# KV times wo in 64x64 tiles for two head groups at once, and modulation rows put beside den

## The chip, the cores and the metric

The kernel runs on one core of one Trainium2 chip. The metric is device time in microseconds (us) of one execution; lower is better. Engines are named as in the profile: PE is the matrix engine, PEld its weight loads, DVE the vector engine, ACT the scalar engine, POOL the GpSimd engine, SP the engine whose queue issues nearly all DMA transfers.

## What is computed

One transformer block on 2048 tokens of width 1024: linear attention with 32 heads of 32, and a gated feed-forward layer of width 3584, each behind a layernorm that six modulation rows (shift, scale and gate for each half) scale and shift. The reference, cut to what matters:

```
mod = silu(c) @ w_mod                      # six rows of 1024: sa ca ga sb cb gb
h = layernorm(x) * (1 + ca) + sa
q, k, v = h @ wqkv                         # 32 heads of 32
phi = lambda t: where(t > 0, t + 1, exp(t)) + 1e-6
kv  = einsum('bhsd,bhse->bhde', phi(k), v) # one 32x32 block for each head
z   = einsum('bhsd->bhd', phi(k))
num = einsum('bhqd,bhde->bhqe', phi(q), kv)
den = einsum('bhqd,bhd->bhq', phi(q), z) + 1e-6
x = x + ga * ((num / den) @ wo)
h = layernorm(x) * (1 + cb) + sb
x = x + gb * ((gelu(h @ w_gate) * (h @ w_up)) @ w_down)
```

## The kernel before

The 2048 tokens are 16 chunks of 128, in four groups of 512. The program is recorded as a list of operations for each engine. PE's and SP's lists keep the order in which the code records them; the lists of DVE, ACT and POOL are put in a new order over the first third of the kernel by `reorder`, a list planner that works with a table of costs (`COST`) by name and starts first what is due first. Operations on one engine run in their list's order, and an operation waits on semaphores for what it depends on. SP has eight lanes: a transfer waits for the transfer eight places before it.

The steps around the change:

- K and Q are computed and put through phi. V is never formed: with M = phi(K)^T h (tiles `m_tile`, L895, 8 head groups of 128 columns, three column parts each), the product KV of a head group g is M times the V weights.
- M is copied to bf16 by ACT (L900), transposed by a DMA into `mtb` (`m_t`, L703; two buffers, so the transpose of group g waits for the KV product of g-2), and multiplied with the V weights by `kv_prod` (L913, 8 matmuls of 128 columns). The result, one 128x128 matrix of which only the four 32x32 blocks on the diagonal belong to heads, is multiplied by a block mask on DVE into `KVT` (L917).
- KV times wo, `w2_pair` (L1196): for each head group, `KVT` of the group (128x128, block diagonal) is the stationary operand and 128 rows of wo the moving one, two matmuls of 512 columns into two PSUM banks. ACT copies the result to bf16, `W2` (L1198). wo itself is loaded by two transfers (`wo_load`) and multiplied beforehand by the gate row ga on DVE (`wofold`, L1202).
- The modulation rows of a later step are summed by `mod_rows` (L840): a matrix of ones as stationary operand, 32 columns wide, four row parts beside each other in the four column quarters of the array (this is what "column-tiled" means below). ACT copies the rows out and SP stores them to DRAM (`mod_store`, L849). sb and cb are read back from there with one value to a partition, `sbT` and `cbT` (L1213), 1024 values of 4 bytes each; `cb1` on DVE (L1749) adds one.
- `den` (L1223) makes the denominators of half of the tokens: 32 matmuls of 32 stationary columns, again four beside each other. DVE adds 1e-6 and takes the reciprocal, SP stores it (L1231), and `rb_load` (L1243) reads it back, spread over the 32 partitions of each head: 256 KB for each of four transfers to a half group. `pq_scale` on DVE (L1256, `pqs`) multiplies phi(Q) with it.
- `wo_mm` (L1266): phi(Q) times `W2`, 16 matmuls for a chunk; DVE adds the result to x (L1274, `x1`).
- The second layernorm's rows are transposed by DMA (L703 into `h2a` and `h2b`), modulated (L724 on DVE, L753 on ACT), and go into the feed-forward layer, which works with sums and differences of blocks (seven products in place of eight): `s_sum` (L1395, `ss`) of the activations, `t_sum` (L1415, `tp`) of the weights `wt`, products L1440.

The table `HOOK` says behind which M tile (0 to 23, `tiles`) each of these steps is recorded. After the tiles a fixed sequence mixes the first chunks of `wo_mm` with the last KV products and the last groups of `w2_pair`; SP's transfers `rb_load(1)` and `rb_load(2, (1,))` are recorded there too. `gb_rows` makes the gate row of the second half, whose stored value is read back much later.

Of the kernel before, what the change touches and what calls it, by code (L numbers as in the profile page):

```python
# [7 lines left out]
ACTF = mybir.ActivationFunctionType  # L8
ALU = mybir.AluOpType

P = 128
# [7 lines left out]
NG = 8  # L19
# [151 lines left out]
class Sched:  # L171
# [41 lines left out]
    def dma(self, stream, fn, rd=(), wr=(), deps=(), note="", overwrite_ok=False):  # L213
# [6 lines left out]
        if prev is not None:  # L220
# [4 lines left out]

    COST = {
        PE_: {"T": (0.056, 0.15), "k": (0.216, 0.15), "q": (0.216, 0.15), "v": (0.216, 0.15), "m": (0.145, 0.15), "kv": (0.056, 0.15), "den": (0.027, 0.15),
              "modr": (0.04, 0.15), "mod": (0.028, 0.15), "w": (0.216, 0.15), "wo": (0.216, 0.15), "ffn": (0.216, 0.15)},
        ACT_: {"exp": (0.5, 0.1), "sum": (1.19, 0.1), "sq": (1.28, 0.1), "xhata": (1.14, 0.1), "hmoda": (0.49, 0.1), "mcp": (0.38, 0.1), "zc": (0.13, 0.1),
               "mhi": (0.52, 0.1), "mrow": (0.4, 0.1), "wcp": (0.92, 0.1), "hraw": (0.92, 0.1), "hmodb": (0.75, 0.1), "arcp": (0.98, 0.1),  # L230
               "brcp": (0.98, 0.1), "pcp": (0.55, 0.1), "escp": (0.55, 0.1), "gelu": (0.55, 0.1)},
        DVE_: {"min": (0.34, 0.085), "add": (0.607, 0.085), "bn": (0.603, 0.085), "aggr": (0.124, 0.085), "ve": (0.07, 0.085), "xhat": (0.46, 0.085),
               "nm": (0.074, 0.085), "hmod": (0.25, 0.085), "macc": (0.66, 0.085), "mlo": (0.6, 0.085), "kvt": (0.21, 0.085), "z": (0.34, 0.085),
               "dene": (0.335, 0.085), "rden": (1.67, 0.085), "pqs": (0.6, 0.085), "wofold": (1.13, 0.085), "x": (1.14, 0.085), "ssum": (1.15, 0.085), "tsum": (1.15, 0.085), "padd": (0.62, 0.085), "yT": (0.62, 0.085)},
        POOL_: {"nmean": (0.22, 0.05), "ve": (0.22, 0.05), "rstd": (0.55, 0.05), "nm": (0.55, 0.05), "ones": (0.12, 0.05), "ssum": (2.3, 0.05), "tsum": (2.3, 0.05)},
        SP_: {"T": (1.25, 1.25), "Tb": (1.25, 1.25), "mT": (1.25, 1.25), "wm": (0.45, 2.9), "wo": (0.45, 2.7), "wv": (0.45, 1.45), "x": (0.45, 2.7), "gab": (0.45, 1.3),
              "sbT": (0.45, 1.3), "cbT": (0.45, 1.3), "rb": (0.45, 1.2), "wt": (0.45, 2.9), "wd": (0.45, 5.8), "wmg": (0.45, 2.9), "gbb": (0.45, 1.3), "rdenst": (0.45, 0.3), "mrowst": (0.45, 0.05)},
# [93 lines left out]
def bass_adaLN_cond__linear_attn_block__geglu_ffn__prompt_kernel(  # L331
# [18 lines left out]
    with ExitStack() as es:  # L350
# [195 lines left out]
        def PS(b, c0=0, c1=512):  # L546
            return ps_all[:, b * 512 + c0: b * 512 + c1]
# [241 lines left out]
        def r_hlg(j, h):  # L789
            return [(OFF_TMP + (2 * j + h) * 1024, OFF_TMP + (2 * j + h + 1) * 1024, "hlg")]  # L790
# [41 lines left out]
        def mod_rows(parts):  # L832
            for k0, n, bank, src in parts:
                o = None
                w = n * P
                for h in range(2):
                    for j in range(4):
                        ap, rng = src(k0 + j * n // 4, h)
                        ap = ap[:, j * w % 512:j * w % 512 + w]
                        o = sch.op(T, lambda e, h=h, j=j, ap=ap, bank=bank, w=w: e.matmul(  # L840
                            ps_all[32 * j:32 * (j + 1), bank * 512:bank * 512 + w], ONES[:, :], ap, start=(h == 0), stop=(h == 1)),
                            rd=rng + r_sm("ones"), pwr=(pr(bank) if h == j == 0 else ()), note=f"modr{k0}.{h}.{j}")
# [66 lines left out]
        def kv_prod(g, bank):  # L909
            i = g % 2  # L910
            o = None
            for dc in range(NDC):
                o = sch.op(T, lambda e, dc=dc: e.matmul(PS(bank, 0, P), WV[:, g, dc, :], MTB[i][:, dc, :],  # L913
                                                        start=(dc == 0), stop=(dc == NDC - 1)),
                           rd=r_wv(g) + r_mtb(i), pwr=(pr(bank) if dc == 0 else ()), note=f"kv g{g} dc{dc}")
# [274 lines left out]
            sch.op(V, lambda e: e.tensor_tensor(Z32[:], BM32[:], ZCOLS[:, :].unsqueeze(2).to_broadcast([P, NG, NH]), ALU.mult),  # L1190
                   rd=r_sm("bm32") + r_sm("zcols"), wr=r_sm("z32"), note="z32")

        def w2_pair(g, b0=6):
            for half in range(2):
                b = b0 + half
                sch.op(T, lambda e, b=b, half=half: e.matmul(PS(b), KVT[:, g, :], WO[:, g, half * 512:(half + 1) * 512], start=True, stop=True),  # L1196
                       rd=r_kvt(g, g + 1) + r_wo(g, half * 512, (half + 1) * 512), pwr=pr(b), note=f"w2 {g}.{half}")
            sch.op(A, lambda e: e.activation(W2[:, g, :], ps_all[:, b0 * 512:(b0 + 2) * 512], ACTF.Copy),  # L1198
                   prd=pr(b0) + pr(b0 + 1), wr=r_w(OFF_WK, "w2", g), note=f"w2cp{g}")

        def wofold(kc):
            sch.op(V, lambda e: e.tensor_tensor(WO[:, kc, :], WO[:, kc, :], GAB[:, :], ALU.mult), rd=r_wo(kc) + R_GAB, wr=r_wo(kc), note=f"wofold {kc}")  # L1202

        def wo_load(j):
            sch.dma(Q, lambda e: e.dma_start(WO[:, 4 * j:4 * j + 4, :], wo_v[:, 4 * j:4 * j + 4, :]),
                    wr=[t_ for g in range(4 * j, 4 * j + 4) for t_ in r_wo(g)], note=f"wo{j}")

        def mod_pass():
            assert mdone[0] >= 48 and not late
            mod_rows(((2, 4, 5, hl_src),))  # L1210
            o_r = mod_store(4, 5, MROW[1], r_2k(OFF_ROW + 2048, "mrow1"), 1)
            for dst, nt, a0 in ((SBT, "sbT", 0), (CBT, "cbT", 2)):
                sch.dma(Q, lambda e, dst=dst, a0=a0: e.dma_start(dst[:, :], scr_row[1, a0:a0 + 2, :].rearrange("a (b p) -> p (a b)", p=P)),  # L1213
                        wr=r_sm(nt), deps=[o_r], note=nt)

        HW = SGW // 2

# [43 lines left out]
        def wo_mm(c_, b0, gs):  # L1261
# [9 lines left out]
            if gs[-1] == NG - 1:  # L1271
# [38 lines left out]
        for n, (g, k) in enumerate(tiles):  # L1310
# [656 lines left out]
```

## Time and profile before

| | |
|---|---|
| median of 3 runs | 783.46 us (783.44 to 783.54) |
| the profiled execution | 783.52 us, of which the span in the trace is 781.7 |
| granted clock of PE | 1.00 |
| PE busy | 774.5 us (99%) |
| DVE, ACT, POOL busy | 641.9, 376.3, 47.0 us |
| M tiles and what is between them | 127.5 to 191.8 us of the span |
| first chunks of `wo_mm` with the last KV products | 191.8 to 200.9 us |
| the remaining chunks to 13 | 200.9 to 242.3 us |
| the feed-forward layer's first unit, with chunks 14 and 15 | 242.3 to 262.0 us |
| end of all PE work | 777.4 us |

How to read the views that are shown: the chain of waits is followed back from the last instruction, at each step to what released it, and printed in order of time; pieces stand end to end. In a timeline each row is a run of like instructions with its start, the time from its first start to its last end, engine, line, operation, tiles written and read, shapes and count, and in brackets the idle time of the engine just before it with what ended it. A matmul's own duration contains its way through the array, so the time that it costs in a row of matmuls is seen from start to start. The table by stretch gives busy time of each engine in a window, then granted clock, DMA share and GB/s. "To landing" is the time from a transfer's issue to the moment when its semaphore is complete. All times are from the start of the span.

### The profile page before, as it was taken

The numbers are of one execution on the slowest core, as the hardware profiler recorded it, in microseconds if no ns is written. First come the engines' busy times: TensorE is split into PE (matmuls) and PEld (weight loads), VectorE is DVE, ScalarE is ACT, GpSimd is POOL, SyncE is SP. The second block draws the span as 40 slices with busy tenths as digits, with TensorE's granted clock in tenths as the row PEclk, the third lists the DMA queues.
The fourth block names the chain that finished last, engine by engine and source line by source line (L and its number), as shares of the span: only waits on it lengthen the run. The fifth ranks groups of instructions, "written<-read, shape, count | busy, mean of one in ns | idle before, by whom it ended". The sixth has DMA issues, their size and how long they took to land.

```text
span 781.7 us, 10762 instructions
## 1 busy us (share of the span) xinstructions
PE 774.5 (99%) x3867; PEld 497.4 (64%) x3867; DVE 641.9 (82%) x954; ACT 376.3 (48%) x631; POOL 47.0 (6%) x126
## 2 busy tenths in 40 slices
PE   8999999999999999999999999999999999999998
PEld 4444445666445667677676767677676576677766
DVE  6699988896689877787989888888989888676767
ACT  2497743243566487778655565555555211111111
POOL 2031300000331012100000000000000000000000
DMA  9879749939999247867353866435356334444331
GB/s 289 250 166 252 156 84 260 229 70 182 216 270 248 82 128 215 226 184 214 93 152 107 246 207 180 141 102 160 94 150 218 112 115 152 145 141 123 113 128 60
DMA packets 196844, 130.22 MB, mean 167 GB/s; under 512 B 69420, under 2 KB 182324, under 8 KB 195768
## 3 DMA queue, kind: packets, MB, share of 16 engines
q1 hardware_dynamic: 196776, 129.55, 61.0%
q8 instruction: 30, 0.49, 0.3%
q14 instruction: 22, 0.18, 0.1%
q10 hardware_dynamic: 16, 0.00, 0.0%
HBM read 92.55 MB, written 23.35 MB: 148 GB/s over the span
## 4 chain that ended last, share of the span: by engine, by line
PE 97%; SPq 1%; DMA 1%; DVE 0%; issue 0%; DVEq 0%
PE ps_all L1440 45%; PE ps_all L1654 21%; PE ps_all L895 7%; PE ps_all L1266 7%; PE ps_all L931 7%; PE ps_all L880 6%; PE ps_all L1575 1%; DMA wmq<-in_w_mod_dram 1%; SPq L598 1%; SPq L603 1%; PE ps_all L913 0%; PE ps_all L1196 0%; SPq L592 0%; PE ps_all L1223 0%; PE ps_all L766 0%; PE ps_all L840 0%
## 5 line engine op out<-in xcount | busy, mean ns | idle before, releaser
L1440 PE MATMUL ps_all<-ss,tp 128*128 128x512 f32 x896 | 214.3, 396 | 0.0
L1440 PEld LDWEIGHTS ps_all<-ss,tp 128*128 128x128 f32 x896 | 168.3, 188 | 37.7 <-DVE ss L1395 0.3
L1654 PE MATMUL ps_all<-dt,sb 128*128 128x512 f32 x424 | 102.5, 398 | 0.0
L1440 PE MATMUL ps_all<-h2a,wt 128*128 128x512 bf16 x448 | 101.6, 380 | 0.0
L1463 ACT ACTIVATE ge<-ps_all 128x512 f32<-128x512 f32 x112 | 64.1, 597 | 73.8 <-DVE ps_all L1451 62.0
L1654 PEld LDWEIGHTS ps_all<-dt,sb 128*128 128x128 f32 x424 | 79.6, 188 | 18.4 <-DVE sb L1630 0.3
L1458 DVE TENSOR_TENSOR ps_all<-ps_all,es 128x512 f32<-128x512 f32 x54 | 37.5, 699 | 49.7 <-ACT es L1448 49.3
L1470 DVE TENSOR_TENSOR ys<-ge,ps_all 128x512 bf16<-128x512 f32 x112 | 74.4, 684 | 3.4 <-PE ps_all L1654 0.5
L1440 PEld LDWEIGHTS ps_all<-h2a,wt 128*128 128x128 bf16 x448 | 37.9, 97 | 57.2 <-ACT ps_all L1445 16.9
L1415 DVE TENSOR_TENSOR tp<-wt 128x1024 fp32r<-128x1024 bf16 x56 | 68.1, 1216 | 2.1 <-DMA wt<-in_B_w_up_dram 2.1
L1415 DVE TENSOR_TENSOR tp<-wt,tp 128x1024 fp32r<-128x1024 bf16 x56 | 68.2, 1219 | 0.0
L880 PE MATMUL ps_all<-wk,h1T 128*128 128x512 bf16 x248 | 56.7, 379 | 0.3 <-DVE h1T L724 0.2
L931 PE MATMUL ps_all<-h1T,wq 128*128 128x512 bf16 x256 | 56.7, 379 | 0.0
L1266 PE MATMUL ps_all<-w,pq 128*128 128x512 bf16 x256 | 56.3, 379 | 0.0
L1440 PE MATMUL ps_all<-ar,tp 128*128 128x512 f32 x224 | 55.5, 390 | 0.0
L869 ACT ACTIVATE eb<-ps_all 128x512 f32<-128x512 f32 x64 | 36.3, 593 | 37.7 <-PE ps_all L880 15.3
L1654 PE MATMUL ps_all<-wd,ya 128*128 128x512 bf16 x212 | 48.5, 380 | 0.0
L1440 PEld LDWEIGHTS ps_all<-ar,tp 128*128 128x128 f32 x224 | 42.1, 188 | 8.8
L1445 ACT ACTIVATE ps_all<-ps_all 128x512 f32<-128x512 f32 x56 | 32.6, 582 | 27.1 <-PE ps_all L1440 27.1
L931 PEld LDWEIGHTS ps_all<-h1T,wq 128*128 128x128 bf16 x256 | 24.9, 98 | 30.0
L1266 PEld LDWEIGHTS ps_all<-w,pq 128*128 128x128 bf16 x256 | 24.7, 98 | 29.9 <-ACT w L1198 0.3
L1625 ACT ACTIVATE sb<-ya 128x896 fp32r<-128x896 bf16 (+1 forms) x16 | 14.5, 913 | 58.8 <-PE ps_all L1654 58.8
(140 smaller groups left out, 977.5 us busy)
## 6 DMA issues: line engine op xcount, KB each, us to landing
wt<-in_B_w_gate_dram SPq DMA_DIRECT2D x28, 512.0 KB, 4.1
wt<-in_B_w_up_dram SPq DMA_DIRECT2D x28, 512.0 KB, 5.3
scr_y<-ys SPq DMA_DIRECT2D x28, 512.0 KB, 3.2
ya<-scr_y SPq DMA_DIRECT2D x14, 896.0 KB, 5.9
rb<-scr_rd SPq DMA_DIRECT2D x32, 256.0 KB, 6.9
wd<-in_B_w_down_dram SPq DMA_DIRECT2D x7, 1024.0 KB, 7.9
wmst<-in_w_mod_dram SPq DMA_DIRECT2D x6, 1024.0 KB, 5.7
wmq<-in_w_mod_dram SPq DMA_DIRECT2D x8, 512.0 KB, 6.8
```

The source lines that it names most:

```text
L869: sch.op(A, lambda e: e.activation(EB[i][:, :], PS(bank), ACTF.Exp), prd=pr(bank), wr=rng, note=f"{note}.exp")
L880: o = sch.op(T, lambda e, dc=dc: e.matmul(PS(bank), H1[sg][:, ci, dc, :], W_[:, dc, jg * 512:(jg + 1) * 512], start=(dc == 0), stop=(dc == ...
L895: o = sch.op(T, lambda e, c_=c_: e.matmul(PS(bank, 0, n), PK[c_][:, g * P:(g + 1) * P], xrow(c_, o_, o_ + n), start=(c_ == 0), stop=(c_ == ...
L931: o = sch.op(T, lambda e, dc=dc: e.matmul(PS(b), WQ[:, dc, qc * P:(qc + 1) * P], H1[sg][:, :, dc, :], start=(dc == 0), stop=(dc == NDC - 1 ...
L1266: last[half] = sch.op(T, lambda e, g=g, half=half: e.matmul(PS(b0 + half), PQ[sg][:, g, ci * P:(ci + 1) * P], W2[:, g, half * 512:(half + ...
L1415: sch.op(V, lambda e: e.tensor_tensor(TP[k][:], in0, in1 if k in (0, 2) else in1[:], ALU.subtract), rd=r0 + r1, wr=r_tp(k), deps=[x1_ops[7 ...
L1440: o = sch.op(T, lambda e, l_=l_, r_=r_, dc=dc: e.matmul(PS(b), l_, r_, start=fresh and dc == 0, stop=dc == ND2 - 1, skip_group_check=True) ...
L1445: sch.op(A, lambda e: e.activation(PS(BB + t), PS(BA + t), ACTF.Copy), prd=pr(BA + t), pwr=pr(BB + t), note="pcp")
L1458: sch.op(V, lambda e: e.tensor_tensor(PS(BC + t), PS(BC + t), ES[t][:, :], ALU.add), prd=pr(BC + t), rd=r_2k(OFF_ES[t], f"es{t}"), pwr=pr( ...
L1463: sch.op(A, lambda e: e.activation(GE[i][:, :], PS(b), ACTF.Gelu_apprx_tanh), prd=pr(b), wr=r_2k(OFF_GE[i], f"ge{i}"), note="gelu")
L1470: sch.op(V, lambda e: e.tensor_tensor(YS[s_][:, 2 * h:2 * h + 2, t, :], q(GE[i][:, :]), q(PS(b + 1)), ALU.mult), rd=r_2k(OFF_GE[i], f"ge{i ...
L1654: o = sch.op(T, lambda e, l_=l_, r_=r_, j=j, dst=dst: e.matmul(dst, l_[:, 0, :], r_, start=(k in (1, 5) or own is not None) and j == js[0] ...
```

## The change

Of a 128x128 `KVT` only the two 64x64 blocks on the diagonal can be other than zero. The changed kernel keeps only these. `kv_prod` masks each of the two blocks by itself on DVE and puts it into `KVT` so that the partitions 0 to 63 hold the blocks of an even group and 64 to 127 those of the odd group beside it. wo is loaded by four transfers of 64 partitions each, so that its rows lie in the same way. `w2_pair(i)` then makes two head groups at once: 8 matmuls of 64x64 tiles with 512 columns each; the two row halves of the array belong to the two groups and write to different banks, the two column halves to the two blocks of a group. It uses four banks (4 to 7) in place of two. Of the last two pairs, DVE makes the second copy to `W2` in place of ACT.

The four pairs stand behind tile 11, behind tile 17, and twice in the sequence after the tiles. The modulation rows of sb and cb (`modp`) stand directly before den0 behind tile 16, where before they stood behind tile 14; the rows of gb (`gbr`) stand directly behind den1 after tile 20, where before they stood behind tile 21, and use bank 7. The reads of `sbT` and `cbT` (`mod_in`) are recorded after `rb_load(1)` and `rb_load(2, (1,))`, where before they followed the store. The planner's cost table has new values for three names.

```diff
-              "modr": (0.04, 0.15), "mod": (0.028, 0.15), "w": (0.216, 0.15), "wo": (0.216, 0.15), "ffn": (0.216, 0.15)},
+              "modr": (0.04, 0.15), "mod": (0.028, 0.15), "w": (0.07, 0.3), "wo": (0.216, 0.15), "ffn": (0.216, 0.15)},
...
-               (DVE) "kvt": (0.21, 0.085)
+               (DVE) "kvt": (0.15, 0.085), "wcp": (1.05, 0.085)
...
         def gb_rows():
-            mod_rows(((0, 2, 5, lambda j, h: (HLG[:, j, h, :], r_hlg(j, h))),))
-            o_gb[0] = mod_store(2, 5, MRG, [(OFF_TMP + 4096, OFF_TMP + 5120, "mrg")], 2)
+            mod_rows(((0, 2, 7, lambda j, h: (HLG[:, j, h, :], r_hlg(j, h))),))
+            o_gb[0] = mod_store(2, 7, MRG, [(OFF_TMP + 4096, OFF_TMP + 5120, "mrg")], 2)
...
             pset_writer(bank, o)
-            sch.op(V, lambda e: e.tensor_tensor(KVT[:, g, :], PS(bank, 0, P), BMASK[:, :], ALU.mult), prd=pr(bank), rd=r_sm("bmask"),
-                   wr=r_kvt(g, g + 1), note=f"kvt{g}")
+            z = 64 * (g % 2)
+            for h in range(2):
+                a, gz = 64 * h, g // 2 * 2 + h
+                sch.op(V, lambda e, a=a, gz=gz: e.tensor_tensor(KVT[z:z + 64, gz, 0:64], ps_all[a:a + 64, bank * 512 + a:bank * 512 + a + 64], BMASK[a:a + 64, a:a + 64], ALU.mult),
+                       prd=pr(bank), rd=r_sm("bmask"), wr=r_kvt(gz, gz + 1), note=f"kvt{g}", overwrite_ok=True)
...
-        def w2_pair(g, b0=6):
-            for half in range(2):
-                b = b0 + half
-                sch.op(T, lambda e, b=b, half=half: e.matmul(PS(b), KVT[:, g, :], WO[:, g, half * 512:(half + 1) * 512], start=True, stop=True),
-                       rd=r_kvt(g, g + 1) + r_wo(g, half * 512, (half + 1) * 512), pwr=pr(b), note=f"w2 {g}.{half}")
-            sch.op(A, lambda e: e.activation(W2[:, g, :], ps_all[:, b0 * 512:(b0 + 2) * 512], ACTF.Copy),
-                   prd=pr(b0) + pr(b0 + 1), wr=r_w(OFF_WK, "w2", g), note=f"w2cp{g}")
+        def w2_pair(i, b0=4):
+            for hf in range(2):
+                for r in range(2):
+                    for h in range(2):
+                        b, g = b0 + 2 * r + hf, 2 * i + h
+                        sch.op(T, lambda e, b=b, g=g, h=h, r=r, hf=hf: e.matmul(ps_all[64 * h:64 * h + 64, b * 512:(b + 1) * 512], KVT[64 * r:64 * r + 64, g, 0:64],
+                               WO[64 * r:64 * r + 64, g, hf * 512:(hf + 1) * 512], start=True, stop=True),
+                               rd=r_kvt(g, g + 1) + r_wo(g, hf * 512, (hf + 1) * 512), pwr=pr(b), note=f"w2 {i}.{hf}", overwrite_ok=True)
+            for r in range(2):
+                b, g = b0 + 2 * r, 2 * i + r
+                w_, p_ = W2[:, g, :], ps_all[:, b * 512:(b + 2) * 512]
+                eng = V if i > 1 and r else A
+                sch.op(eng, lambda e, w_=w_, p_=p_, eng=eng: e.activation(w_, p_, ACTF.Copy) if eng == A else e.tensor_copy(w_, p_),
+                       prd=pr(b) + pr(b + 1), wr=r_w(OFF_WK, "w2", g), note=f"w2cp{g}")
...
         def wo_load(j):
-            sch.dma(Q, lambda e: e.dma_start(WO[:, 4 * j:4 * j + 4, :], wo_v[:, 4 * j:4 * j + 4, :]),
-                    wr=[t_ for g in range(4 * j, 4 * j + 4) for t_ in r_wo(g)], note=f"wo{j}")
+            for r in range(2):
+                wo_ops.append(sch.dma(Q, lambda e, r=r: e.dma_start(WO4[64 * r:64 * r + 64, :, j, :], wo_rows[r, :, :, j, :]),
+                                      wr=() if r else [t_ for g in range(j, NG, 2) for t_ in r_wo(g)], deps=wo_ops[-1].deps if r else (), note="woe"))
...
         def mod_pass():
-            mod_rows(((2, 4, 5, hl_src),))
-            o_r = mod_store(4, 5, MROW[1], r_2k(OFF_ROW + 2048, "mrow1"), 1)
+            mod_rows(((2, 4, 6, hl_src),))
+            o_sb[0] = mod_store(4, 6, MROW[1], r_2k(OFF_ROW + 2048, "mrow1"), 1)
+
+        def mod_in():
             for dst, nt, a0 in ((SBT, "sbT", 0), (CBT, "cbT", 2)):
                 sch.dma(Q, lambda e, dst=dst, a0=a0: e.dma_start(dst[:, :], scr_row[1, a0:a0 + 2, :].rearrange("a (b p) -> p (a b)", p=P)),
-                        wr=r_sm(nt), deps=[o_r], note=nt)
+                        wr=r_sm(nt), deps=[o_sb[0]], note=nt)
...
-        HOOK = {0: "ga", 6: "kv0", 8: "w0", 9: "kv1", 11: "w1", 12: "kv2", 14: "w2 modp", 15: "kv3 z32", 16: "den0", 17: "w3 rb0.0 rb0.1", 18: "",
-                19: "kv4", 20: "w4 den1 ps0.0", 21: "gbr", 22: "ps0.1", 23: "rb2.0"}
+        HOOK = {0: "ga", 6: "kv0", 9: "kv1", 11: "w0", 12: "kv2", 15: "kv3 z32", 16: "modp den0", 17: "w1 rb0.0 rb0.1", 18: "",
+                19: "kv4", 20: "den1 gbr ps0.0", 22: "ps0.1", 23: "rb2.0"}
...
-        E6 = list(range(6))
-        wo_mm(0, 0, E6[:5])
-        w2_pair(5)
+        wo_mm(0, 0, [0, 1, 2, 3])
+        w2_pair(2)
+        wo_mm(1, 2, [0, 1, 2])
         kv_prod(6, 4)
-        wo_mm(1, 2, E6[:5])
         kv_prod(7, 5)
-        w2_pair(6)
-        wo_mm(0, 0, E6[5:])
-        wo_mm(1, 2, E6[5:])
+        wo_mm(0, 0, [4, 5])
         rb_load(1)
         rb_load(2, (1,))
-        wo_mm(2, 4, E6[:4])
-        w2_pair(7)
-        wo_mm(2, 4, E6[4:])
+        mod_in()
+        w2_pair(3)
+        wo_mm(1, 2, [3, 4, 5])
+        wo_mm(2, 4, list(range(6)))
         for c_ in range(3):
             wo_mm(c_, 2 * c_, [6, 7])
```

More of the change, by code (lines that the diff above doesn't have):

```diff
@@ L232 @@
         DVE_: {"min": (0.34, 0.085), "add": (0.607, 0.085), "bn": (0.603, 0.085), "aggr": (0.124, 0.085), "ve": (0.07, 0.085), "xhat": (0.46, 0.085),
-               "nm": (0.074, 0.085), "hmod": (0.25, 0.085), "macc": (0.66, 0.085), "mlo": (0.6, 0.085), "kvt": (0.21, 0.085), "z": (0.34, 0.085),
-               "dene": (0.335, 0.085), "rden": (1.67, 0.085), "pqs": (0.6, 0.085), "wofold": (1.13, 0.085), "x": (1.14, 0.085), "ssum": (1.15, 0.085), "tsum": (1.15, 0.085), "padd": (0.62, 0.085), "yT": (0.62, 0.085)},
+               "nm": (0.074, 0.085), "hmod": (0.25, 0.085), "macc": (0.66, 0.085), "mlo": (0.6, 0.085), "kvt": (0.15, 0.085), "z": (0.34, 0.085),
+               "dene": (0.335, 0.085), "wcp": (1.05, 0.085), "rden": (1.67, 0.085), "pqs": (0.6, 0.085), "wofold": (1.13, 0.085), "x": (1.14, 0.085), "ssum": (1.15, 0.085), "tsum": (1.15, 0.085), "padd": (0.62, 0.085), "yT": (0.62, 0.085)},
         POOL_: {"nmean": (0.22, 0.05), "ve": (0.22, 0.05), "rstd": (0.55, 0.05), "nm": (0.55, 0.05), "ones": (0.12, 0.05), "ssum": (2.3, 0.05), "tsum": (2.3, 0.05)},
@@ L1201, in wofold @@
         def wofold(kc):
-            sch.op(V, lambda e: e.tensor_tensor(WO[:, kc, :], WO[:, kc, :], GAB[:, :], ALU.mult), rd=r_wo(kc) + R_GAB, wr=r_wo(kc), note=f"wofold {kc}")
+            sch.op(V, lambda e: e.tensor_tensor(WO[:, kc, :], WO[:, kc, :], GAB[:, :], ALU.mult), rd=r_wo(kc) + R_GAB, wr=r_wo(kc), deps=wo_ops[2 * (kc % 2) + 1:2 * (kc % 2) + 2], note=f"wofold {kc}")
+        wo_ops = []
+        WO4 = WO[:].rearrange("p (i h) d -> p i h d", h=2)
+        wo_rows = A_wo.rearrange("(i r h p) d -> r p i h d", r=2, h=2, p=64)
@@ L1208, in mod_pass @@
         def mod_pass():
             assert mdone[0] >= 48 and not late
-            mod_rows(((2, 4, 5, hl_src),))
-            o_r = mod_store(4, 5, MROW[1], r_2k(OFF_ROW + 2048, "mrow1"), 1)
+            mod_rows(((2, 4, 6, hl_src),))
+            o_sb[0] = mod_store(4, 6, MROW[1], r_2k(OFF_ROW + 2048, "mrow1"), 1)
+        o_sb = [None]
+        def mod_in():
             for dst, nt, a0 in ((SBT, "sbT", 0), (CBT, "cbT", 2)):
                 sch.dma(Q, lambda e, dst=dst, a0=a0: e.dma_start(dst[:, :], scr_row[1, a0:a0 + 2, :].rearrange("a (b p) -> p (a b)", p=P)),
-                        wr=r_sm(nt), deps=[o_r], note=nt)
+                        wr=r_sm(nt), deps=[o_sb[0]], note=nt)
```

## The prediction

> **What bounds the kernel now.** I read four views: busy times, then the chain that ended last, then the SP queue and the DMA share, then DVE's and PE's order of time where PE meets DVE.
>
> ```profile
> PE 774.5 (99%) x3867; PEld 497.4 (64%) x3867; DVE 641.9 (82%) x954; ACT 376.3 (48%) x631; POOL 47.0 (6%) x126
> ```
>
> PE is busy 99%. From the chain of waits, in order of time (start, us, what), around the edited instructions:
>
> ```profile
> 165.16 0.43 PE ps_all L1196 x2
> 165.59 0.55 PE ps_all L840 x8
> 166.14 2.43 PE ps_all L895 x16
> 168.56 0.45 PE ps_all L913 x8
> 169.01 2.32 PE ps_all L895 x16
> 171.33 0.99 PE ps_all L1223 x32
> 172.32 2.43 PE ps_all L895 x16
> ```
>
> These stand end to end, so a PE microsecond saved here is one gained here. One head group's KV times wo (L1196) costs 0.43. The column-tiled stretches cost more than their stream: the modulation rows (L840, 8 matmuls of 512 columns, four side by side, so two rounds) take 0.55 where two full-width matmuls of 512 take 0.43, and the 16 matmuls behind take 2.43, not 2.32. So a stretch costs 0.23 beyond its stream, and den (L1223) shows about the same.
>
> Whether the gain reaches the end is decided later. The SP queue's timeline:
>
> ```profile
> 173.70 0.37 SPq L1213 DMA_DIRECT2D sbT<-scr_row  x1
> 174.12 0.58 SPq L1213 DMA_DIRECT2D cbT<-scr_row  x1
> ...
> 192.09 1.25 SPq L703 DMA_TRANSPOSE mtb<-mb  x1
> 193.45 12.44 SPq L1243 DMA_DIRECT2D rb<-scr_rd  x16
> 210.76 1.24 SPq L703 DMA_TRANSPOSE h2a<-xl  x1
> ```
>
> The two small loads have an idle queue at 174; at 193 sixteen loads of 256 KB begin, and transposes and weights follow. Table by stretch (the last three columns are the granted clock, DMA share and GB/s):
>
> ```profile
> 195.00:205.00 10.00, 10.00 (x54) 4.67 (x52) 4.64 (x8) 3.14 (x4) 0.22 (x1) 1.00 1.02 230
> 205.00:214.00 9.00, 9.00 (x43) 4.09 (x42) 9.00 (x16) 6.46 (x11) 5.90 (x12) 1.00 1.01 214
> ```
>
> The DMA engines are full in both. Then DVE:
>
> ```profile
> 214.04 0.16 DVE L1749 TENSOR_SCALAR cb1T<-cbT 128x8 f32<-128x8 f32 x1
> 214.92 1.22 DVE L1274 SCALAR_TENSOR_TENSOR xall<-ps_all,xall 128x1024 bf16<-128x1024 f32 x1 [0.72 <-PE ps_all L1266]
> ...
> 225.33 1.22 DVE L1415 TENSOR_TENSOR tp<-wt 128x1024 fp32r<-128x1024 bf16 x1 [2.11 <-DMA wt<-in_B_w_up_dram]
> ...
> 251.65 1.21 DVE L1395 TENSOR_TENSOR ss<-h2a,h2b 128x1024 fp32r<-128x1024 bf16 x1
> ```
>
> and PE:
>
> ```profile
> 249.48 3.63 PE L1266 MATMUL ps_all<-w,pq 128*128 128x512 bf16 x16
> 252.92 2.12 PE L1440 MATMUL ps_all<-ss,tp 128*128 128x512 f32 x8
> ```
>
> DVE waits 2.11 for a weight transfer, then runs almost without a pause from 225.33 to 252.86, where it ends the ss that PE takes at 252.92. No room is left: what feeds DVE at 225 to 231 by DMA sets PE at 253. The first ss,tp products begin at 245.61; the second eight (245.61 + 8 x 0.225 = 247.4) need the ss ending at 246.99, a room of 0.4.
>
> **The change, part by part.** The sum is made against the profiled execution: 783.52 us, of which the span is 781.7 and 1.8 lie around it; the median of the runs is 783.46, 0.06 less.
>
> KV times wo. Removed: 8 pairs x 0.43 = 3.44. Added: 4 stretches of 8 matmuls of 64 x 64. If four run at once (two row halves into different PSUM banks, two column halves), that is two rounds of 512, as L840: 0.43 of stream + 0.23 = 0.66, times 4 = 2.64. No row has tiles of 64 rows. Bounds: 0.66 (all four at once), 1.09 (column halves only, four rounds), 1.94 (one after the other). I take 0.66, since L840 is the nearest row: four tiles, 512 columns. The larger ends are a rival below.
>
> Joint stretches. Modulation rows directly before den0, and den1 directly before the other rows, are one column mode each: 2 x 0.23 = 0.46 saved. PE's sum: -3.44 + 2.64 - 0.46 = **-1.26**. By the last KV product of the tile loop (191.4 before) the same 1.3 is already won: five pairs gone (-2.15), two stretches added (+1.32), -0.46.
>
> On loading weights, the row first: in L1223's stretch 32 loads of 128x32 go beside 32 matmuls in 0.99, and eight rounds of 256 columns are 0.85 of that, so the second load of a tile isn't in the open. The Trainium skill (TensorE: Matmul & The Clock Gate, "The mechanism") says that a weight load overlaps running matmuls only when its row group differs; den's tiles all share theirs, so the trace disagrees. By that rule the second round of each new stretch would pay a load of 0.1 in the open, PE's sum would be about -0.9, and the rival in which all is kept would end at 782.6.
>
> DVE, ACT. Each bmask product becomes two of 64x64 (nearest row 0.28 for 128x128, 8 more: between 0 and 2.2 in all), and two of the eight W2 copies move from ACT (1.02 each) to DVE (nearest row 1.22). Cover: from 192.4 to 200.9 DVE does 0.6 of work in 8.5. Behind the copies in DVE's queue stand the KVT products of groups 6 and 7: copy 193.0 to 194.2, group 7's second product ends near 195.8, the last w2 stretch wants it at 196.1. ACT's copies free the banks: kv6 wants bank 4 at 194.2, the copy ends near 194.0; chunk 2 wants it at 198.0, the copy ends near 197.8. Rooms of 0.2 to 0.3, taken as nothing; without them 0.1 to 0.5 is lost.
>
> DVE's planned order also changes: mlo7 lies between kv4's products and den1's sum. Adding the rows from dene0 on, it ends near 182.0 and PE wants it at 182.9.
>
> Queues. wo comes in four loads of 64 partitions instead of two. SP's two issues took 3.0; gab behind them is issued at 136.9. If 64 partitions load at the rate of the rb loads (1.2 per 256 KB of 32 partitions), 2 MB take 9.4 instead of about 6, gab comes 4 later, and DVE, first needing it at 140.9, has idle rows of 1.57, 1.29 and 0.98 to catch up, while the first w2 moves from 149.3 to 156.7. I take 0; the other end is 0.5.
>
> mrow1's store, rden0's store and mT4 move up with PE; the rb loads then begin near 176.5, not 177.56, so the transpose mT5 (landed 9.1 after 181.43, at 190.5) lands near 189.4, and kv5 wants it at 190.1. mT7 can go only after kv5: it lands 3.1 after its issue, near 193.9, wanted at 194.7. mrow2's store now stands before mT6, which has over 2 of room. POOL's order is unchanged.
>
> The loads sbT and cbT move behind rden0's store, mT4, the first eight rb loads, mT5, rden1's store, mT6, mT7 and the sixteen rb loads, ahead of the first h2a transpose. Their price in the trace, for the two (174.8 to 176.4, hardly anything else in the queue):
>
> ```profile
> q1 hardware_dynamic: 2075, 0.01, 73.2%
> ```
>
> 73.2% of 1.6 is 1.17 of all sixteen engines for 8 KB. At 174 that was idle time; now it stands in the full stretch, so the transposes, weights and rb loads behind come 1.17 later than the shift of -1.26 alone would have them: **-0.1** against before. Bounds: 0 (the queue has gaps there) and 3.1 (each load's time to landing, if the transposes wait for it). I take 1.17, the engine time. cb1 on DVE then waits for cbT to about 215.3 instead of starting at 212.8; behind it on DVE stand x1 of chunk 5, four pqs, x1 of 6, eight h2 products and x1 of 7, 8 in all, which end near 223.4. The wait for wt until 225.2 swallows that.
>
> So PE arrives 1.26 early and waits: ss1 and ss2 come only 0.1 earlier, and PE loses about 1.1 at 247 and 253. Behind, chunk 15's second matmul waited some 0.15 for ys (ends 255.07), which hangs on DVE being free after chunk 14; with PE later than DVE there that goes too. Sum: -1.26 + 1.17 - 0.15 = -0.24. 783.52 - 0.24 - 0.06 = 783.2; I say **783.1**, since the gaps of the queue can only lower the give-back of 1.17.
>
> **The rivals.** (1) All of it is kept: the small loads fit the queue's gaps, as when a transpose waits for its predecessor (SP stands 5.75 on two of them at 213.03, and from 214 to 216 only 70 GB/s are moved). Against it, the shares of 1.02 and 1.01. PE -1.26: 782.2; where a new stretch costs 0.55, as L840's own row has it, -1.7: 781.8. (2) The queue costs more than was gained: the h2a transpose begins only when cbT has landed, 3.1 behind the last rb load; DVE's 225 to 253 starts later than before and PE waits. -1.26 + 3.1 = +1.8: 785.3. For: transposes stand long at issue there (5.75 for two). Against: mT5 was issued in 1.23 with eight rb loads under way. It decides for slower from a give-back of 1.26 on, and beyond what can be told from no change from 2.83. (3) The 64 x 64 tiles don't run beside each other by rows: 4 x 0.43 = 1.7 more, PE +0.45, 783.9; one after the other, 4 x 1.28 more, PE +3.9, 787.4. Nothing in the trace excludes it; den's four columns side by side speak against the second. (4) A new wait on PE. Behind kv5 (mT7, copies, KVT products) one of up to 1 is swallowed by PE's later waiting. Ahead of it, as when mT5 lands no earlier than 190.5 or later, it delays mT7 and with it the sixteen rb loads: 1 to 2 on top of -0.24, 784.2 to 785.2.
>
> **How the numbers follow.** A difference under 0.2% (1.57 us) is about what a measurement of this kernel can't tell from none: 781.9 to 785.0. Forecast, mostly handed back: 0.42, wholly inside. (1) 0.29, of which 0.15 below 781.9. (2) 0.15, of which 0.07 above 785.0. (3) 0.07, 0.03 above. (4) 0.07, 0.04 above. Faster 0.15, same 0.71, slower 0.14. The range 781.8 to 784.9 leaves out about 0.06 below and 0.14 above.
>
> **What would show it.** The two-group products: 4 stretches of about 0.55 with 0.1 before and behind; if they last 1 or more, (3). KV product 5 near 190.1 instead of 191.4. cb1 with a wait on cbT, and ss1 and ss2 within 0.3 of 246.99 and 252.86 by the clock of the span, with PE idle or stretched ahead of L1440's ss,tp near 247 and 253; if ss comes 1 earlier, (1); if later than before, (2). Wrong it would be by a transpose that stands behind the small loads for longer than 1.2, or by a queue that takes them for nothing.

## The result and the profile after

The changed kernel takes 786.29 us (median of 5 runs, 785.38 to 787.01) beside 783.44 for the kernel before: a ratio of 1.0036, with a 95% interval of 1.0025 to 1.0046. It is slower by 2.85, outside the range that was forecast. The profiled execution took 787.01, with a span of 785.2; the granted clock is 1.0 throughout. Busy time of each engine, from the page of the changed kernel:

```profile
PE 774.9 (99%) x3883; PEld 496.2 (63%) x3883; DVE 645.5 (82%) x964; ACT 374.4 (48%) x629; POOL 47.7 (6%) x126
```

PE's busy time is 774.9 where it was 774.5, though work was taken out: part of a wait is booked as busy (the one ahead of KV product 1 is 1.52 in the brackets below and 1.68 by the starts). So the totals don't tell where the time went. It is seen in PE's order of time. First the changed kernel, then the kernel before (start, us, instruction, and in brackets the idle time ahead of it and what ended it):

```profile
145.09 0.61 PE L913 MATMUL ps_all<-mtb,wv 128*128 128x128 bf16 x8 [0.52 <-issue]
...
154.18 0.62 PE L913 MATMUL ps_all<-mtb,wv 128*128 128x128 bf16 x8 [1.52 <-DMA mtb<-mb]
...
172.53 0.61 PE L840 MATMUL ps_all<-hl,ones 128*32 128x512 bf16 x8
172.98 1.05 PE L1242 MATMUL ps_all<-pq,z 128*32 128x256 bf16 x32
173.96 1.19 PE L895 MATMUL ps_all<-xrow,pk 128*128 128x342 bf16 x7
174.98 1.47 PE L895 MATMUL ps_all<-xall,pk 128*128 128x342 bf16 x9
176.38 0.63 PE L1201 MATMUL ps_all<-wo,kvt 64*64 64x512 bf16 x8
176.94 1.19 PE L895 MATMUL ps_all<-xrow,pk 128*128 128x342 bf16 x7
...
192.66 0.61 PE L913 MATMUL ps_all<-mtb,wv 128*128 128x128 bf16 x8
...
248.13 2.11 PE L1457 MATMUL ps_all<-ss,tp 128*128 128x512 f32 x8 [0.55 <-DVE xall L1293]
250.41 2.11 PE L1457 MATMUL ps_all<-ss,tp 128*128 128x512 f32 x8 [0.16 <-DVE ss L1412]
...
256.28 2.10 PE L1457 MATMUL ps_all<-ss,tp 128*128 128x512 f32 x8 [0.29 <-DVE ss L1412]
...
265.35 3.63 PE L1457 MATMUL ps_all<-h2a,wt 128*128 128x512 bf16 x16
```

```profile
144.22 0.61 PE L913 MATMUL ps_all<-mtb,wv 128*128 128x128 bf16 x8
...
152.07 0.61 PE L913 MATMUL ps_all<-mtb,wv 128*128 128x128 bf16 x8
...
191.37 0.61 PE L913 MATMUL ps_all<-mtb,wv 128*128 128x128 bf16 x8
...
262.03 3.63 PE L1440 MATMUL ps_all<-h2a,wt 128*128 128x512 bf16 x16
```

Two things are to be seen. The new matmuls cost what was forecast: the 64x64 stretch runs from 176.38 to 176.94, 0.56, and starts 0.09 behind the end of the M tile ahead (174.98 and nine matmuls of 0.145 make 176.29), 0.65 in all where 0.66 was forecast; modulation rows and den together take 1.43 from 172.53 to 173.96. But PE now waits in two places where it did not: for the transposes mT0 and mT1 ahead of KV products 0 and 1 (145.09 and 154.18), and for DVE at 248 (an x1), 250 and 256 (ss sums).

To set the two apart I cut the span at three starts: of the tile loop's first M product, of KV product 5 (192.66; 191.37 before), and of the second FFN unit's first product (265.35; 262.03 before). The first cut lies 0.18 later. From it to KV product 5, called A below, the changed kernel needs 64.95 instead of 63.85 (+1.10); from there to the second FFN unit, called B, 72.69 instead of 70.66 (+2.03); the rest +0.16. The sum is 3.47, the difference of the spans.

A's wait begins on SP. The queue of the changed kernel, then of the kernel before:

```profile
127.73 2.77 SPq L1220 DMA_DIRECT2D wo<-in_A_wo_dram  x4
131.09 0.62 SPq L849 DMA_DIRECT2D scr_row<-mrowa  x1
139.76 0.35 SPq L855 DMA_DIRECT2D gab<-scr_row  x1
140.23 1.32 SPq L703 DMA_TRANSPOSE mtb<-mb  x1
...
143.90 5.57 SPq L703 DMA_TRANSPOSE mtb<-mb  x1
```

```profile
126.90 3.02 SPq L1205 DMA_DIRECT2D wo<-in_A_wo_dram  x2
130.90 0.64 SPq L849 DMA_DIRECT2D scr_row<-mrowa  x1
136.94 0.35 SPq L855 DMA_DIRECT2D gab<-scr_row  x1
137.39 1.29 SPq L703 DMA_TRANSPOSE mtb<-mb  x1
...
142.63 2.49 SPq L703 DMA_TRANSPOSE mtb<-mb  x1
```

The load of gab waits until the store of the row that it reads has landed, and that store stands behind wo. It goes out 2.8 later, and with it everything that SP holds behind it: mT0 first. mT1 leaves only 1.27 later, but stands 5.57 at issue instead of 2.49 and lands at 154.1 instead of 150.2. The reason that gab is late is the rate of the wo loads. By stretch (length, the five engines' busy time, granted clock, DMA share, GB/s), first of the kernel before, with 128 partitions:

```profile
131.00:136.00 5.00, 5.00 (x37) 3.34 (x35) 5.00 (x8) 1.32 (x3) 0.00 (x0) 1.00 0.97 370
```

then of the changed kernel, with 64:

```profile
131.00:138.00 7.00, 7.00 (x50) 4.64 (x48) 7.00 (x13) 1.96 (x7) 0.00 (x0) 1.00 1.07 226
```

The DMA engines are full in both and move 370 and 226 GB/s. The Trainium skill (SBUF — State Buffer, "Door 1: The DMA port swizzle (why `[64,N]` ≈ `[32,N]`)") says that 64 neighbouring partitions lie behind only half of the 16 ports, so that such a transfer goes no faster than one of 32. The trace agrees in kind: 226 here is near the 230 of the rb loads of 32 partitions, and 0.61 of the rate of 128.

B's wait begins on SP too. The changed kernel, then the lines of the kernel before that the prediction did not show:

```profile
207.71 0.39 SPq L1232 DMA_DIRECT2D sbT<-scr_row  x1
208.94 1.01 SPq L1232 DMA_DIRECT2D cbT<-scr_row  x1
212.11 5.12 SPq L703 DMA_TRANSPOSE h2a<-xl  x1
217.28 0.58 SPq L592 DMA_DIRECT2D xall<-in_A_x_dram  x1
217.95 4.32 SPq L703 DMA_TRANSPOSE h2a<-xl  x2
222.32 0.57 SPq L1370 DMA_DIRECT2D wt<-in_B_w_gate_dram  x1
```

```profile
212.05 0.58 SPq L592 DMA_DIRECT2D xall<-in_A_x_dram  x1
213.03 5.75 SPq L703 DMA_TRANSPOSE h2a<-xl  x2
218.83 0.57 SPq L1353 DMA_DIRECT2D wt<-in_B_w_gate_dram  x1
```

The h2a transpose behind the small loads stands at issue for 5.12 instead of 1.24; the first wt goes out 29.66 behind KV product 5 instead of 27.46. DVE's wait for wt moves with it:

```profile
218.23 0.17 DVE L1766 TENSOR_SCALAR cb1T<-cbT 128x8 f32<-128x8 f32 x1 [2.65 <-DMA cbT<-scr_row]
...
228.54 1.23 DVE L1432 TENSOR_TENSOR tp<-wt 128x1024 fp32r<-128x1024 bf16 x1 [1.72 <-DMA wt<-in_B_w_up_dram]
```

From 228.54 on (225.33 before) DVE has no room, and PE's second FFN unit comes 3.32 later than before.

### The profile page after: what moved, and what is told of

It is laid out like the page before. It is cut to its first block, busy times and chain, and to the rows that moved or that the text cites. A ratio compares the mean times of both kernels' runs of the same rounds, so it can differ in the third digit from the quotient of the medians.

```text
span 785.2 us, 10801 instructions
## 1 busy us (share of the span) xinstructions
PE 774.9 (99%) x3883; PEld 496.2 (63%) x3883; DVE 645.5 (82%) x964; ACT 374.4 (48%) x629; POOL 47.7 (6%) x126
## 4 chain that ended last, share of the span: by engine, by line
PE 88%; DMA 5%; DVE 3%; SPq 3%; issue 1%; ACT 1%; DVEq 0%; ACTq 0%
PE ps_all L1457 44%; PE ps_all L1671 21%; PE ps_all L934 7%; PE ps_all L895 4%; PE ps_all L880 4%; PE ps_all L1285 4%; PE ps_all L1592 1%; DMA mtb<-mb 1%; SPq L598 1%; DMA scr_row<-mrowa 1%; DMA wmq<-in_w_mod_dram 1%; DVE ss L1412 1%; DMA rb<-scr_rd 1%; SPq L603 1%; DVE xall L1293 1%
```

## The experiments

The theory after the result, called theory A in the expectations (A and B alone are the two stretches above): the two losses are separate and add up, the four wo loads through gab and the transposes behind it, the two small loads through the h2a transpose behind them. All runs below were timed beside the kernel before, which took 783.19, 783.24 and 783.39 in the three groups (single runs between 782.5 and 784.6); each time is to be compared with that of its group. The table has each kernel's own profiled execution cut as above (in us; "rest" is from the second FFN unit to the end). The start of the tile loop wanders by 1.6 from profile to profile, so A and B say more than the span.

| kernel | start | A | B | rest | span | time (median) | ratio to before, 95% |
|---|---|---|---|---|---|---|---|
| before | 127.52 | 63.85 | 70.66 | 519.70 | 781.7 | 783.44 | |
| changed | 127.70 | 64.95 | 72.69 | 519.86 | 785.2 | 786.29 | 1.0036 (1.0025 to 1.0046) |
| 1 small loads early | 127.14 | 64.25 | 71.55 | 519.76 | 782.7 | 784.11 | 1.0012 (1.0003 to 1.0020) |
| 2 wo in 128 partitions | 126.89 | 62.58 | 72.65 | 520.26 | 782.4 | 784.27 | 1.0016 (1.0008 to 1.0025) |
| 3 both | 126.93 | 62.57 | 71.14 | 519.68 | 780.3 | 782.50 | 0.9992 (0.9983 to 1.0001) |
| 4 before, small loads late | 127.56 | 63.84 | 73.69 | 520.01 | 785.1 | 785.56 | 1.0033 (1.0020 to 1.0046) |
| 5 before, wo in four | 127.10 | 64.97 | 70.69 | 519.69 | 782.4 | 785.79 | 1.0027 (1.0016 to 1.0039) |
| 6 small loads from ACT | 126.67 | 63.50 | 71.55 | 519.67 | 781.4 | 784.13 | 1.0013 (1.0003 to 1.0022) |
| 7 half of them late | 127.58 | 65.33 | 72.79 | 519.79 | 785.5 | 787.20 | 1.0041 (1.0028 to 1.0053) |
| 8 mended, halves behind mT1 | 128.26 | 66.57 | 71.67 | 519.77 | 786.3 | 787.53 | 1.0056 (1.0043 to 1.0069) |
| 9 late in 128 packets each | 127.02 | 64.38 | 70.71 | 519.69 | 781.8 | 784.01 | 1.0007 (0.9998 to 1.0016) |
| 10 mended, small behind mT6 | 127.70 | 62.58 | 71.11 | 519.71 | 781.1 | 782.71 | 0.9991 (0.9983 to 1.0000) |
| 11 mended, small behind mT5 | 127.77 | 62.58 | 71.20 | 519.73 | 781.3 | 782.51 | 0.9991 (0.9982 to 1.0000) |

**1. The small loads early.**

```diff
         rb_load(2, (1,))
-        mod_in()
...
-                19: "kv4", 20: "den1 gbr ps0.0", 22: "ps0.1", 23: "rb2.0"}
+                19: "kv4 sc", 20: "den1 gbr ps0.0", 22: "ps0.1", 23: "rb2.0"}
...
+            elif f == "sc":
+                mod_in()
```

> The changed kernel with one thing put back: sbT and cbT are loaded behind the transpose mT5, ahead of rden1's store, where SP's queue stood idle from 184.4 to 188.2. Theory A: the change loses in two places that add up: the four wo loads hold up gab and with it the transposes mT0 and mT1 behind it (PE waits of 0.7 and 1.7 at KV products 0 and 1, 2.4), and the two small loads behind the rb loads cost the stretch from 207 to 229 about 1.9 over what PE's delay explains. Then this run keeps the first loss and drops the second: KV product 5 stays near 192.6, cb1 no longer waits, the first wt lands near 226.5 instead of 228.35, and the time falls by about 1.9 from 786.3 to 784.4. Rival B: the transposes and weights behind the rb loads are late for PE's delay and the transposes' own issue alone; the small loads only happen to stand there, and the time stays within 0.5 of 786.3.

Measured 784.11, 0.92 above its kernel before, where the changed kernel was 2.85 above: 1.9 less. B falls from 72.69 to 71.55, the h2a transpose goes in 1.23, and the ss,tp products run without the pauses at 248 and 250. B stays 0.89 above the kernel before; here the sixteen rb loads begin 2.97 behind KV product 5 instead of 2.06, since cbT now stands 5.54 at issue ahead of mT6 and mT7, and PE pauses 0.36 for a pq product at 208.70. Rival B (the small loads only happen to stand there) is out. A keeps its waits for mT0 and mT1: 64.25 against the 62.57 of experiment 3.

**2. wo in two loads of 128 partitions.**

```diff
...
-            for r in range(2):
-                wo_ops.append(sch.dma(Q, lambda e, r=r: e.dma_start(WO4[64 * r:64 * r + 64, :, j, :], wo_rows[r, :, :, j, :]),
-                                      wr=() if r else [t_ for g in range(j, NG, 2) for t_ in r_wo(g)], deps=wo_ops[-1].deps if r else (), note="woe"))
+            sch.dma(Q, lambda e: e.dma_start(WO[:, 4 * j:4 * j + 4, :], wo_v[:, 4 * j:4 * j + 4, :]),
+                    wr=[t_ for g in range(4 * j, 4 * j + 4) for t_ in r_wo(g)], note=f"wo{j}")
```

> The changed kernel with wo loaded in two loads of 128 partitions as before (the rows then stand in the wrong places for the 64x64 products, so that the output isn't the reference's; every instruction on the engines is the same). Theory A: 2 MB land near 137 instead of 139.8, gab is issued near 137, mT0 lands near 142, the waits of 0.7 and 1.7 at KV products 0 and 1 are gone, KV product 5 comes near 190.2, and the time falls by about 2.4 from 786.3 to 783.9. Rival C: the waits at KV products 0 and 1 come from elsewhere (DVE's or ACT's order, gab's chain) or are given back behind, since the sixteen rb loads and what follows are bound by the DMA engines: the time falls by less than 0.8.

Measured 784.27. From SP's queue:

```profile
134.92 0.34 SPq L855 DMA_DIRECT2D gab<-scr_row  x1
...
141.99 1.25 SPq L703 DMA_TRANSPOSE mtb<-mb  x1
```

The waits ahead of KV products 0 and 1 are gone, and A is 62.58: 1.27 under the kernel before, where the prediction had 1.3 won by KV product 5. B stays at 72.65, so what A gains over the changed kernel is not given back in B, and rival C is out.

**3. Both.** The two diffs above together.

> Both of the former: small loads early, wo in two loads of 128 partitions (rows of wo in the wrong places). Theory A: the losses are gone and PE's -1.25 is left: 783.44 - 1.25 = 782.2, with KV product 5 near 190.2 and the ss,tp products at 252.92 before near 251.7. Rival B or C: above 783.4. If the h2a transposes and wt come no earlier for other reasons, between 782.6 and 783.4.

Measured 782.50, 0.69 under the kernel before, with an interval that just takes in no change. A 62.57, B 71.14. The queue of this kernel:

```profile
208.93 1.23 SPq L703 DMA_TRANSPOSE h2a<-xl  x1
...
217.26 0.57 SPq L1370 DMA_DIRECT2D wt<-in_B_w_gate_dram  x1
```

By its time beside those of experiments 1 and 2, the four loads cost 1.6 (784.11 - 782.50) and the small loads 1.8 (784.27 - 782.50). Of A's 1.27, 0.48 is lost again in B. PE pauses 0.24 at 206.38 for a pq product; where the small loads come early, DVE has two of these products ahead of the first x1 instead of three. What the rest of the 0.48 is, no run shows.

**4. The kernel before, with the small loads late.** `mod_in()` split off from `mod_pass` and called behind `rb_load(2, (1,))`, as in the change.

> The kernel before with one thing of the change: sbT and cbT are loaded behind the sixteen rb loads. Theory A: KV product 5 stays at 191.4, the first wt lands 1.9 later than 225.14, near 227.0, and the time rises from 783.44 to about 785.3 (784.6 if the loads cost only their engine time of 1.17, as the prediction had it). Rival B: it stays within 0.3 of 783.44.

Measured 785.56, 2.37 above its kernel before. A is untouched (63.84), B is 3.03 longer, and the transpose stands 6.13. From SP's queue in this kernel:

```profile
207.68 0.43 SPq L1218 DMA_DIRECT2D cbT<-scr_row  x1
210.80 6.13 SPq L703 DMA_TRANSPOSE h2a<-xl  x1
```

So the move of two loads of 4 KB costs most of what the whole change cost, alone. The 1.17 of the prediction is too little.

**5. The kernel before, with wo in four loads.** In `wo_load`, rows 64r to 64r+63 of each half by a load of their own, as in the change, but to the old places.

> The kernel before with one thing of the change: wo in four loads of 64 partitions instead of two of 128 (same bytes, same places). Theory A: 64 partitions take 2.2 to 2.3 per 512 KB, as in the changed kernel, so the last lands 2.5 later, gab is issued near 139.5, and mT0 and mT1 behind it land near 144.5 and 153: waits at KV products 0 and 1 of together 1.7 to 2.4, KV product 5 that much later than 191.4, and the time 1.7 to 2.4 above the kernel before. Rival C: DVE and PE catch up, as the prediction had it: within 0.5 of the kernel before.

Measured 785.79, 2.55 above its kernel before. Here B is the kernel before's (70.69) and A is longer. From SP's queue, gab and mT0 behind it:

```profile
139.13 0.35 SPq L855 DMA_DIRECT2D gab<-scr_row  x1
139.59 1.32 SPq L703 DMA_TRANSPOSE mtb<-mb  x1
```

The profiled execution was the fastest of its six (784.27 to 786.16) and shows only 1.12 in A; the waits for mT0 and mT1 differ from execution to execution (A is 0.9 to 2.8 above 62.57 in the profiles of kernels 1, 6, 7, 9 and the changed one). Rival C, the prediction's own reading, is out.

**6. The small loads from ACT's queue.** They are issued at 197.9 and 198.4, in the middle of the sixteen rb loads, with nothing of SP's behind them.

```diff
-                sch.dma(Q, lambda e, dst=dst, a0=a0: e.dma_start(dst[:, :], scr_row[1, a0:a0 + 2, :].rearrange("a (b p) -> p (a b)", p=P)),
-                        wr=r_sm(nt), deps=[o_sb[0]], note=nt)
+                sch.dma(A, lambda e, dst=dst, a0=a0: e.dma_start(dst[:, :], scr_row[1, a0:a0 + 2, :].rearrange("a (b p) -> p (a b)", p=P)),
+                        wr=r_sm(nt), deps=[o_sb[0], w2c[A]], note=nt)
```

(`w2c[A]` is ACT's last copy of W2, and `mod_in()` stands behind `w2_pair(3)`.)

> The changed kernel with the two small loads issued from ACT's queue, near 200.5, in the middle of the sixteen rb loads: their packets still go through the sixteen full DMA engines, but nothing stands behind them on SP. Theory A1 (what costs is SP standing at the h2a transpose until the queue ahead of it has drained): the transpose that stood 5.1 at issue goes in 1.2, wt lands as in the run with the small loads early, and the time is 784.1 to 784.5. Theory A2 (what costs is the engine time of the small packets, 1.17, as the prediction had it): the last rb loads land 1.2 later and the time is near 785.3. If the packets cost more than that in any place, near 786.3.

Measured 784.13, as in experiment 1, and the transpose goes in 1.24 (209.77 to 211.01). From SP's queue:

```profile
209.77 1.24 SPq L703 DMA_TRANSPOSE h2a<-xl  x1
...
218.58 0.57 SPq L1372 DMA_DIRECT2D wt<-in_B_w_gate_dram  x1
```

By the time, theory A1 holds against A2: the same packets in the same full stretch cost 1.1 less in B when SP need not stand behind them. But the engine time is there too: the last rb load lands 25.4 behind KV product 5, where it landed 24.1 behind it in the changed kernel, the first wt goes out 28.42 behind it (27.46 in the kernel before), and B is still 0.89 above the kernel before. So of the 2.0 that B lost, SP's standing carries 1.1; the engine time may carry much of the rest, and this run doesn't say how much.

**7. Only cbT late.** sbT goes behind mT5.

> The changed kernel with sbT loaded behind mT5 and cbT alone behind the rb loads: half the small packets. If the price goes by the packets, half of the 2.2 that both cost comes back: 785.2. If it is a question of whether the queue is full when the transpose comes, it is either nearly all there (786) or nearly gone (784.3). By the engine time alone: 784.1 + 0.6 = 784.7.

The time, 787.20, cannot be read for this: the profile's waits for mT0 and mT1 are the longest of all (A 2.76 above 62.57). B is 72.79, as with both late, the transpose stands 3.97, and the first wt goes out 29.68 behind KV product 5, as in the changed kernel. But sbT early also makes the rb loads begin 0.5 later against KV product 5, and PE pauses 0.64 for a pq product at 210.21. So whether half the packets cost half is not shown.

**8. Both losses mended, first try.** The loads of wo's odd slots behind mT1, the folds in the order 0 2 4 6 1 3 5 7, the small loads as in experiment 1.

> The changed kernel, complete, with both losses mended: the loads of wo's second halves stand behind the transpose mT1 instead of ahead of gab (the products of wo and gab in the order 0 2 4 6 1 3 5 7), and the small loads behind mT5. Theory A: no waits at KV products 0 and 1, and the time of the run with both losses undone, 782.5, some 0.7 under the kernel before. Rival: the loads behind mT1 hold up mT2, which KV product 2 wants 8 after KV product 1, or the second fold, which the first 64x64 stretch wants: then PE waits near 156 to 159 and the time is 783 to 784.

Measured 787.53: the rival's case, and more of it. From PE's order of time:

```profile
159.00 0.63 PE L1201 MATMUL ps_all<-wo,kvt 64*64 64x512 bf16 x8 [1.38 <-DVE kvt L920]
...
164.45 0.61 PE L913 MATMUL ps_all<-mtb,wv 128*128 128x128 bf16 x8 [2.39 <-ACT w L1208]
```

The first 64x64 stretch needs slots 0 and 1 (a slot is the place of one head group's rows in the wo tile), and slot 1 is now loaded late. DVE's fold of it waits 6.28 for the load, until 155.89; the mask products of group 1 stand behind that fold on DVE and start at 158.47, and PE waits for them. KV product 2 behind waits for the bank that ACT copies out late. A grows to 66.57.

**9. The small loads late, in fewer packets.**

```diff
-                sch.dma(Q, lambda e, dst=dst, a0=a0: e.dma_start(dst[:, :], scr_row[1, a0:a0 + 2, :].rearrange("a (b p) -> p (a b)", p=P)),
+                sch.dma(Q, lambda e, dst=dst, a0=a0: e.dma_start(dst[:, :], scr_row[1, a0:a0 + 2, :].rearrange("a (q b) -> (a q) b", b=8)),
```

> The changed kernel with the two small loads at the same late place, as 128 packets of 32 bytes each instead of 1024 of 4 (the values then stand in the wrong cells of sbT and cbT, so that the output isn't the reference's). Theory A1: what costs is the number of packets that stand in the queue ahead of the h2a transpose; with 256 instead of 2048 it goes in near 1.3 as before, the first wt is issued 0.7 to 1.2 earlier against KV product 5 and more, and the time is 784.1 to 784.6. Rival D: what costs is that cb1, and DVE's products behind it, wait until cbT has landed behind the last rb load; that wait stays, and so does the time, 785.7 to 786.5.

Measured 784.01, 0.62 above its kernel before: 2.2 less than the changed kernel. Same place, same bytes, same queue; SP's order of time in this kernel:

```profile
207.89 0.34 SPq L1232 DMA_DIRECT2D cbT<-scr_row  x1
210.87 1.25 SPq L703 DMA_TRANSPOSE h2a<-xl  x1
...
218.96 0.57 SPq L1370 DMA_DIRECT2D wt<-in_B_w_gate_dram  x1
```

and on DVE:

```profile
216.62 0.17 DVE L1766 TENSOR_SCALAR cb1T<-cbT 128x8 f32<-128x8 f32 x1 [2.23 <-DMA cbT<-scr_row]
...
225.24 1.23 DVE L1432 TENSOR_TENSOR tp<-wt 128x1024 fp32r<-128x1024 bf16 x1 [0.56 <-DMA wt<-in_B_w_up_dram]
```

B is 70.71, the kernel before's within 0.05: the price of the move is wholly gone. cb1's wait on cbT stays at 2.23 and costs nothing, since the wait for wt behind it shrinks to 0.56; rival D is out. What cost was the number of packets in that place, 2048 of 4 bytes; the same 8 KB there in 256 packets cost nothing. Fewer packets take less engine time too, so this run alone does not part the standing from the engine time; experiment 6 does so in part.

**10 and 11. Both losses mended, second try.** wo's first four slots in four loads at the old place, the last four behind mT2 with their folds later; the small loads behind mT6 or mT5.

```diff
...
-        wo_load(0)
-        wo_load(1)
+        wo_load(0)
...
+            if n == 8:
+                wo_load(1)
-            if 2 <= n <= 9:
-                wofold(n - 2)
+            if 2 <= n <= 5 or 11 <= n <= 14:
+                wofold(n - 2 if n < 6 else n - 7)
```

> The changed kernel, complete, with both losses mended otherwise: wo's rows of the first four groups are loaded at the old place, those of the other four behind mT2 (folds 4 to 7 later), and the small loads behind mT6, where the first eight rb loads have drained. Theory A: no waits at KV products 0 to 2, KV product 5 some 62.6 after the tile loop's start (63.85 before), the first wt's issue some 27.5 to 27.8 behind KV product 5, and the time 0.7 to 1.2 under the kernel before. Rival: the loads behind mT2 delay mT3 or the folds and PE waits at KV product 3 or the second 64x64 stretch: no faster than before.

> The same with the small loads behind mT5 instead of mT6, where the second of them stood 5.5 at issue in the run with both losses undone. If that stand delays nothing that counts, the same time as with the loads behind mT6; if it delays mT6, mT7 and the rb loads, 0.3 to 0.6 more.

Measured 782.71 and 782.51, 0.7 and 0.9 under the kernel before, both ratios 0.9991 with an interval up to 1.0000. A is 62.58 in both, as with wo in 128 partitions. The place of the small loads makes no difference that counts. This is the change with its gain kept, less the 0.45 and 0.54 by which B is longer than before; it is at the edge of what the timing can tell from no change.

## Why the prediction was wrong

**PE's sum, -1.26: right.** A falls by 1.27 where PE doesn't wait (63.85 to 62.58 in experiment 2); the prediction had 1.3 of its sum won by KV product 5. The stretch price of 0.66 and the 0.46 of the joint stretches held, and PE has no wait at the places for which rooms were named (mT5, mT6, the copies, the bmask products). Rival (3) is out. An estimate by the Trainium skill's rule on weight loads (TensorE: Matmul & The Clock Gate, "The mechanism") would have been about -0.9; the trace disagrees with it here as it did in den's stretch.

**"I take 0; the other end is 0.5", for wo in four loads: wrong, 1.6 to 2.6.** The delay was foreseen, if a little large: wo slower by about 3.4, gab 4 later (2.8 measured). What failed is that I followed gab to DVE alone, which did catch up, and not the instructions behind gab on its own queue. mT0 and mT1 stand there, and in the kernel before mT0 landed at 141.89 for a KV product at 144.22: a room of 2.3 that a delay of 4, my own figure, was bound to break. This loss falls ahead of KV product 5, in the place of rival (4), but through wo, which that rival didn't name; 190.1 for KV product 5 became 192.66.

**The give-back of 1.17: too small, since a part of the mechanism was left out.** The small loads cost 1.8 (experiments 2 and 3) to 2.4 (experiment 4), inside the bounds of 0 and 3.1. I took the engine time that the packets occupy and nothing else. That time is at most the smaller part (experiment 6). The part left out, 1.1 in B, is that SP stands at the h2a transpose, the place that rival (2) named; and the whole price goes with the number of packets (experiment 9), not with cbT's landing. Rival (2)'s own sign came: ss1 and ss2 end at 250.35 and 256.22, where they ended at 246.99 and 252.86. The row that I set against it, mT5 issued in 1.23 with eight rb loads under way, says little on this: an rb load of 256 KB is 32 packets of 8 KB (195 to 205 in the kernel before: 409 packets, 2.30 MB, of which 128 are small), eight are 256, and the two small loads are 2048.

**cb1's wait is swallowed: right.** It waited 2.65, and 2.23 in experiment 9, where the time shows nothing of it.

**The term of 0.15 for ys: too large.** From the ss,tp products ahead of chunk 15 to those behind it PE took 5.28 before (252.92 to 258.20) and 5.22 after (256.28 to 261.50).

**The sum.** -1.27 in PE, +2.37 in the waits for mT0 and mT1, +2.03 in B, +0.34 at the two ends make 3.47 in the profiled executions (2.85 by the medians). Both terms that I mis-sized erred the same way, and the range treated (2) and (4) as cases that exclude each other. They came together, each worth more than the gain of 1.27.

## What to carry to other kernels

A load that gets slower or is moved has two sets of followers: those who read it, and those who merely stand behind it, or behind whatever waits for it, on its queue; list both, with the room that each has, before a price of nothing is written down. Count the packets of a transfer, not its bytes: a column load of 4-byte elements belongs where the queue is empty, or in a form with fewer packets (experiment 9 times such a form, but its values lie in the wrong cells; a kernel would have to store the rows to suit). And a layout that pleases the matmul, here halves of 64 partitions, has to be paid by the loads that fill it.

## What the runs showed of the hardware

A load to 64 partitions moved 226 GB/s with the DMA engines' share at 1.07, one to 128 partitions 370 at 0.97, with the same rows of 2 KB; two such loads with complementary halves, one behind the other in the queue, did not run side by side.

A transpose behind 2048 packets of 4 bytes stood 5.1 to 6.1 at issue, behind 1024 of them 4.0, behind 256 of 32 bytes 1.25, each time with the last rb loads still under way. Transposes also stood long without such packets (mT1 for 5.57 in the changed kernel, 1.25 in experiment 2). This looks like a queue that takes a limited number of packets; the limit itself was not measured.

Eight 64x64 matmuls of 512 columns run in 0.56, which is two rounds of four side by side and the stretch's overhead: row halves into different PSUM banks and column halves do run at once.
